# Two tiles of pair 0's exps turned by block transposes and transfers, a new search of the order, and 28 idle products in place of 16

## The chip, the cores and the metric

The kernel runs on one core of a Trainium2 chip. A time is the device time of one execution in microseconds; the value compared is the median of several runs. The engines are TensorE (PE), VectorE (DVE), ScalarE (ACT), GpSimd (POOL) and SyncE (SP), which issues most transfers.

## What is computed

Attention on 2 x 8 heads, then two expert layers, everything in 32-bit floats. Cut to what matters:

```python
def _attn_ref(q, k, v):                      # q, k, v: 2 x 8 x 1152 x 64
    q_pool = q.reshape(B, H, S // 2, 2, D).mean(axis=3)
    scores = scale * np.matmul(q_pool, k.transpose(0, 1, 3, 2))
    scores = scores - np.max(scores, axis=-1, keepdims=True)
    attn = np.exp(scores)
    attn = attn / (np.sum(attn, axis=-1, keepdims=True) + 1e-09)
    return np.matmul(attn, v)

def _moe_ref(x, w_in, w_out):                # 1152 x 512, 2048 wide
    h = x @ w_in
    return (np.maximum(h, 0.0) + np.log1p(np.exp(-np.abs(h)))) @ w_out

def _moe2_ref(x, w_gate, w_val, w_out, rms_g):   # 1536 wide
    xn = x / np.sqrt(np.mean(x * x, axis=-1, keepdims=True) + 1e-06) * rms_g
    g = xn @ w_gate
    return (g * (1.0 / (1.0 + np.exp(-g))) * (xn @ w_val)) @ w_out
```

## The kernel before

The sixteen heads are worked as eight pairs, 0 to 7, of heads A and B. After pooling a head has 576 queries: four tiles of 128 (x = 0 to 3) and half a tile; the half tiles of both heads make one mixed tile (x = 4, NF in the code). For each tile `qk` computes the scores against all 1152 keys (six matmuls of 384 columns, nine for the mixed tile), into one of two PSUM buffers, `sA` and `sB`: each head has one, so its next scores wait until the exps of the last are done. `softmax` takes the maximum of each row on VectorE (line 751) and the exps with their sum on ScalarE (line 753). A head's exps go into a ring of two buffers `p`.

The product with v (`av`, line 838) needs the exps with the keys on the partitions, so each tile is turned, in one of two ways. `flip` (line 773) transposes nine blocks of 128x128 for each head on TensorE, into the two-buffer ring `t` in PSUM, and ScalarE or VectorE copies them out (line 372 or 374). `stream` (line 810) does it for the tiles named in `STREAMS`: VectorE transposes each 128x1152 tile of exps in blocks of 32x32 into `turned`, and SyncE's queue then moves the blocks to their partitions in `moved`, in sixteen transfers (line 818) that are issued when the last of the pair's streamed tiles has been turned. The products of streamed tiles are put into the next pair (`before` in the main loop): tile 1 behind its tile 2, tile 3 behind its tile 3. Before the change pairs 1 to 5 stream tiles 1 and 3, pair 6 streams tile 1, pairs 0 and 7 none.

`heat` issues transposes of the identity that nobody reads: `WARM` of them at the start, `WAKE` behind the first scores (line 1286). `prep` loads, pools and splits a pair's q and k into high and low halves (`kk`, `kh`, `qh`, `ql`, `qm`), one pair ahead. The first weights of the expert layers are loaded and split during attention as well. `seven` and `expand` (line 953, 1019 to 1040) and `main_out` (line 1462) are the expert layers' matmuls.

Operations are recorded first (`plan.op`), each with the engines that may do it. The issue order and the engine of each stand in `ORDER`, a table that a search outside of the program wrote: `p46` is operation 46 on TensorE, `v3` operation 3 on VectorE, `a`, `g`, `s` stand for ScalarE, GpSimd and SyncE. `Plan.order` goes through this table and checks that each operation stands behind what it depends on. The durations beside the engines, as in

```python
def act(n, sbuf=True):
    return "ACT", n * 0.00096 + 0.15 if sbuf else n * 0.00085 + 0.155
```

served the search; the program itself uses only the engines' names.

Of the kernel before, what the change touches and what calls it, by code (L numbers as in the profile page):

```python
# [55 lines left out]
WAKE = 16  # L56
# [7 lines left out]
    a147 p152 a149 v79 v74 s214 p150 v75 p155 a151 s61 a156 p157 v83 v153 p159 a158 g221 p162 v160 p164 a154 g222 g223 v195 a161 s219 v239 v163 v235 s218 p186
    p188 v224 a165 a187 v225 p191 v240 v189 g237 p193 a192 p205 v226 a190 p209 v194 g231 v206 g230 p207 v210 g228 p212 a208 p246 a213 g232 a211 p249 v247 g236
    s332 s331 a241 v244 a248 s220 p251 v242 a233 g238 p254 v252 a250 p256 a255 g229 p259 a253 v257 g227 v260 a258 p265 v234 p261 v196 a171 p263 p288 a264 v266
    g338 s197 a262 g339 s217 p268 g337 v289 a269 s335 a243 p291 v245 a290 s330 s201 v270 s334 a267 p293 s198 v292 s199 p296 v294 a355 p298 s200 a297 p300 a299
    v271 a295 p303 v314 s278 v301 a168 p305 s279 p307 a306 s276 a304 v351 a302 p310 s282 p312 v308 g202 s286 g353 s277 a311 v313 s274 a309 p321 v315 p325 s275
    s280 v172 a322 p323 s281 v356 v326 g203 a324 p328 p362 s285 a329 g354 s283 p365 v363 a327 s273 g352 s287 s272 a364 v340 v341 s284 p367 g204 s316 g347 a342
    p372 v368 g346 a366 g344 p370 v373 p375 a371 g348 a376 p377 a369 v360 s320 s319 s317 v361 a374 p379 s479 p383 s478 v378 a380 s318 v416 p381 v343 p386 p406  # L70
    a387 v357 v384 g417 a382 p409 a359 v349 v407 g345 s477 v358 a408 v350 p411 v388 a410 p420 v485 a412 s333 a385 g484 s336 g415 g486 p423 v421 p425 g414 a424
    s481 a426 s482 p430 v389 p427 a422 v428 s396 a431 p452 s399 p454 a453 s390 v461 v169 a429 s400 p457 v455 p459 s405 a458 s392 v498 s398 p468 a460 a456 p470
    v502 s395 v413 p472 v469 g499 s397 a471 s391 p475 v473 p509 g501 a476 s402 s394 p512 g500 v510 a474 s393 s403 v462 a511 s404 p514 s401 v503 v489 s463 a418
    p517 v515 g492 a513 p519 a518 g490 p522 a516 v520 p524 v507 a523 s466 a487 v488 a521 p526 v494 p530 v525 g493 v508 a527 p528 p533 a529 p553 v531 g495 a534
    g491 a504 s601 a496 p556 v554 s467 a506 s602 s464 v505 a555 v170 s600 p558 v497 a557 v173 a532 v535 p563 s483 a180 s465 g608 p566 a559 v564 s480 p568 g607
    a567 p570 g609 a569 v536 s604 a565 p573 s605 v584 g174 s549 a625 v571 p575 a574 a178 s547 p577 g175 a576 s541 g562 v626 p580 a572 v578 g560 s539 p582 s550
    g561 s551 v581 a579 g176 p595 s542 v610 s543 p591 g179 v596 a182 p632 s548 a583 s544 v592 p593 g177 a597 s546 v633 p598 g181 s538 s540 a594 p637 v599 a621
    s537 g183 p635 s545 v638 s552 a634 v611 v617 p642 a636 v618 a639 v585 p640 p645 v643 g616 a641 p653 g624 s726 a646 s586 a184 p647 v630 a612 v419 a644 g185
    p649 v648 p651 v650 s588 a619 v654 p656 g614 s727 p676 a657 a652 s433 g623 s590 p679 a629 v677 s589 g615 s432 s587 v631 a678 p681 v613 a655 v620 v658 p688
# [1580 lines left out]
```

## Time and profile before

| | us |
|---|---|
| median of 3 runs | 650.23 (649.9 to 651.69) |
| the profiled execution | 647.97 |
| its span | 646.2 |
| TensorE busy | 628.1 (97%) |
| VectorE busy | 491.1 (76%) |
| ScalarE busy | 385.6 (60%) |
| GpSimd busy | 155.6 (24%) |

The span runs from the first to the last instruction in the profile; 1.8 us of the execution lie around it. The busy shares are means over stages of different kinds: attention until about 232 us, then the two expert layers, and 4 us of last copies and stores. "Idle before" in brackets behind a row is the time for which the engine waited, with what ended the wait as the profile infers it.

### The profile page before, as it was taken

How to read it: one execution, taken by the hardware profiler on the slowest of the kernel's cores; microseconds unless marked ns; L12 is line 12 of the kernel's file. 1: busy time of each engine (PE TensorE's matmuls, PEld its weight loads, DVE VectorE, ACT ScalarE, POOL GpSimd, SP SyncE). 2: the span in 40 equal slices, each digit the busy share in tenths (PEclk: the TensorE clock that was granted, in tenths of full speed). 3: DMA queues.
4: the chain of work that ended last, by engine and by line, in shares of the span. 5: the costliest groups of instructions: out<-in, count | busy, mean ns of one | idle time of the engine just before them, and what ended most of it. 6: DMA issues, size and time to landing. Idle time of an engine off the chain costs nothing.

```text
span 646.2 us, 10956 instructions
## 1 busy us (share of the span) xinstructions
PE 628.1 (97%) x4286; PEld 535.8 (83%) x4286; DVE 491.1 (76%) x695; ACT 385.6 (60%) x642; POOL 155.6 (24%) x160
## 2 busy tenths in 40 slices
PE   8998999899999999999999999999999999999997
PEld 7987888788888987888888888888888888888886
DVE  7799988989998788897886666878978877765111
ACT  6778777877877775675565554456365645533211
POOL 1442633643246241000001111301200101124201
PEclk9999999999999999999999999999999999999999
DMA  9246776968564214423141111111133133201004
GB/s 257 76 130 169 177 198 152 222 173 229 161 153 131 85 46 152 169 92 130 66 152 43 66 65 65 66 66 60 71 131 130 66 131 109 87 5 61 1 0 147
DMA packets 24850, 72.55 MB, mean 112 GB/s; under 512 B 5279, under 2 KB 6110, under 8 KB 24798
## 3 DMA queue, kind: packets, MB, share of 16 engines
q1 hardware_dynamic: 24222, 71.32, 36.9%
q8 instruction: 34, 0.56, 0.4%
q10 hardware_dynamic: 576, 0.53, 0.2%
q14 instruction: 18, 0.15, 0.1%
HBM read 56.46 MB, written 2.39 MB: 91 GB/s over the span
## 4 chain that ended last, share of the span: by engine, by line
PE 86%; DMA 4%; SPq 3%; ACT 3%; DVE 3%; issue 1%; ACTq 0%; DVEq 0%
PE s L953 24%; PE t L838 10%; PE s L1462 9%; PE s L737 9%; PE t L773 6%; PE t L953 5%; SPq L818 3%; PE s L1020 3%; PE s L1021 3%; PE s L1019 3%; PE t L1462 3%; PE s L1040 2%; PE t L1040 2%; PE t L1066 2%; ACT p L753 1%; PE s L1066 1%
## 5 line engine op out<-in xcount | busy, mean ns | idle before, releaser
L751 DVE TENSOR_REDUCE nm<-s 128x1 f32<-128x1152 f32 x72 | 96.7, 1349 | 17.7 <-PE s L737 14.7
L753 ACT ACTIVATE p<-s,nm 128x1152 f32<-128x1152 f32 x72 | 88.1, 1224 | 17.8 <-DVE nm L751 14.8
L372 ACT CAST areaLR<-areaKF 128x512 fp32r<-128x512 f32 (+2 forms) x55 | 44.4, 822 | 34.2 <-PE s L1462 12.0
L773 PE MATMUL t<-ident,p 128*128 128x128 f32 x378 | 55.7, 277 | 5.1 <-ACT p L753 4.0
L377 POOL TENSOR_TENSOR areaLR<-areaKF,areaLR 128x512 fp32r<-128x512 f32 (+1 forms) x9 | 13.1, 1455 | 173.3 <-ACT areaLR L372 150.4
L773 PEld LDWEIGHTS t<-ident,p 128*128 128x128 f32 x378 | 43.3, 140 | 13.2 <-ACT p L753 6.0
L442 ACT ACTIVATE areaKF<-areaKF 128x1024 f32<-128x1024 f32 (+1 forms) x37 | 39.8, 1079 | 20.6 <-DMA areaKF<-in_w2o_dram 5.1
L377 DVE TENSOR_TENSOR areaKF<-areaKF 128x256 f32<-128x256 f32 (+1 forms) x98 | 48.6, 513 | 2.2 <-ACT areaKF L1146 1.4
L372 ACT CAST areaMR<-areaKF 128x512 fp32r<-128x512 f32 (+1 forms) x37 | 26.6, 719 | 38.6 <-PE t L1462 17.1
L377 POOL TENSOR_TENSOR kk<-kr,kk 64x384 fp32r<-64x384 f32 x39 | 40.0, 1036 | 36.6 <-DVE kk L374 15.4
L453 DVE SCALAR_TENSOR_TENSOR areaKF<-areaKF 128x1024 int32<-128x1024 int32 (+1 forms) x37 | 41.8, 1133 | 3.7 <-ACT areaKF L442 3.3
L372 ACT COPY ptwhole<-t 128x512 f32<-128x512 f32 (+1 forms) x62 | 32.5, 546 | 14.1 <-PE t L773 13.6
L372 ACT CAST areaKR<-areaKF 128x1024 fp32r<-128x1024 f32 (+2 forms) x44 | 36.2, 840 | 6.0 <-DVE areaKF L453 4.7
L838 PE MATMUL t<-areaKF,v 128*64 128x128 f32 x576 | 34.7, 274 | 4.5 <-ACT ptwhole L372 2.0
L953 PE MATMUL s<-areaKR,areaLR 128*128 128x512 f32 x132 | 38.2, 395 | 0.0
L953 PE MATMUL s<-areaKR 128*128 128x512 f32 x130 | 37.9, 397 | 0.0
L838 PEld LDWEIGHTS t<-areaKF,v 128*64 128x64 f32 x576 | 31.5, 137 | 7.0 <-ACT ptwhole L372 2.4
L953 PE MATMUL s<-areaMR,areaKR 128*128 128x512 f32 x134 | 36.9, 393 | 0.0
L377 DVE TENSOR_TENSOR areaLR<-areaKF,areaLR 128x1024 fp32r<-128x1024 f32 (+2 forms) x29 | 29.5, 1028 | 8.3 <-ACT areaLR L372 8.1
L838 PE MATMUL t<-ptwhole,v 128*64 128x128 f32 x576 | 35.0, 275 | 0.0
L838 PEld LDWEIGHTS t<-ptwhole,v 128*64 128x64 f32 x576 | 31.1, 137 | 3.5 <-issue 2.5
L377 DVE TENSOR_TENSOR areaLR<-areaKF,areaMR 128x512 fp32r<-128x512 f32 (+1 forms) x21 | 17.5, 837 | 19.9 <-ACT areaMR L372 19.9
(286 smaller groups left out, 1590.7 us busy)
## 6 DMA issues: line engine op xcount, KB each, us to landing
areaKF<-areaKF SPq DMA_DIRECT2D x80, 144.0 KB, 3.0
areaKF<-in_w_dram SPq DMA_DIRECT2D x16, 512.0 KB, 5.4
areaKF<-in_w1o_dram SPq DMA_DIRECT2D x16, 512.0 KB, 4.6
qr<-in_qT_dram SPq DMA_DIRECT2D x28, 288.0 KB, 4.7
areaKF<-in_wv_dram SPq DMA_DIRECT2D x12, 512.0 KB, 4.1
areaKF<-in_wg_dram SPq DMA_DIRECT2D x12, 512.0 KB, 3.8
areaKF<-in_w2o_dram SPq DMA_DIRECT2D x12, 512.0 KB, 4.2
v<-in_v_dram SPq DMA_DIRECT2D x16, 288.0 KB, 5.2
```

The costliest lines, as they stand in the source:

```text
L372: nc.scalar.copy(out, in_)
L377: engines[e].tensor_tensor(out=out, in0=in0, in1=in1, op=o)
L442: o = op([act(n)], lambda e, x0=x0, x1=x1: nc.scalar.activation(out=word(1, x0, x1).bitcast(F32), in_=word(1, x0, x1).bitcast(F32), scale= ...
L453: op([dve(n)], lambda e, x0=x0, x1=x1: nc.vector.scalar_tensor_tensor(out=word(1, x0, x1), in0=word(1, x0, x1), scalar=3, in1=word(0, x0, ...
L737: nc.tensor.matmul(sc()[:, c, :N], lhsT=q()[:, cut], rhs=k()[:, c * N:(c + 1) * N], start=(i == 0), stop=(i == len(todo) - 1))
L751: u["mx"] = op([dve(S, psum=True)], lambda e: nc.vector.tensor_reduce(out=nm(), in_=sc()[:, :, :N], axis=AX.XY, op=ALU.max, negate=True), ...
L753: o = op([("ACT", 1.42)], lambda e: nc.scalar.activation(out=pr(), in_=sc()[:, :, :N], func=AF.Exp, bias=nm(), accum_out=s["den"]()[:, col ...
L773: nc.tensor.transpose(t()[:, i * P:(i + 1) * P], pr[:, c * P:(c + 1) * P], ident)
L838: nc.tensor.matmul(t()[h * D:h * D + D, :n], lhsT=s["v"][h]()[:, c, :], rhs=rhs, start=(c == 0), stop=(c == CK - 1))
L953: nc.tensor.matmul(bank(), lhsT=a(k), rhs=b(k), start=start and k + i == 0, stop=stop and k + i == 3, skip_group_check=seeded)
L1040: nc.tensor.matmul(out, lhsT=x()[:, cut], rhs=w[:, k], start=k + i == 0, stop=k + i == KC + 1)
L1462: nc.tensor.matmul(out[m](), lhsT=w, rhs=g(), start=j + i == 0, stop=last and j == js[-1] and i == 2)
```

## The change

Pair 0 now streams its tiles 1 and 3 as pairs 1 to 5 do. 36 transposes on TensorE (378 to 342 at line 773) and ten evictions go; four block transposes on VectorE (22 to 26 at line 810) and sixteen transfers of 144 KB (80 to 96 at line 818) come; the products of these two tiles move into pair 1. `WAKE` goes from 16 to 28. The durations for ScalarE and GpSimd are written anew, the third entry of two VectorE durations goes, and `ORDER` is another table throughout: GpSimd has 23 operations more (165 to 188 instructions), of which eight are in the attention stage. The `(3,)` in `STREAMS` and `old[0]` in place of 1 have no effect on the program, since pair 0 is in `DOUBLE` and the one pair with a single streamed tile has tile 1.

```diff
-DOUBLE = (1, 2, 3, 4, 5)
-STREAMS = {pb: (1, 3) if pb in DOUBLE else (1,) if pb else () for pb in range(NP)} | {NP - 1: ()}
+DOUBLE = (0, 1, 2, 3, 4, 5)
+STREAMS = {pb: (1, 3) if pb in DOUBLE else (1,) if pb else (3,) for pb in range(NP)} | {NP - 1: ()}
...
-WAKE = 16
+WAKE = 28
...
-    p46 v3 s10 q11 v8 v4 s12 v7 q13 a45 v9 v5 s14 s15 s16 v20 v21 s17 v2 a22 v6 s18 a28 v23 s19 v29 p48 a24 a44 v25 p47 v26 v27 p49 a32 v34 a30 p54 v50 a35 s57
...
 def act(n, sbuf=True):
-    return "ACT", n * 0.00096 + 0.15 if sbuf else n * 0.00085 + 0.155
+    return "ACT", n * 0.00083 + 0.2 if sbuf else n * 0.00085 + 0.155
...
 def pool(n):
-    return "POOL", 0.05 + n * 0.00275
+    return "POOL", 0.18 + n * 0.0022
...
-            op([("DVE", 1.37, 1)], lambda e, h=h, pr=pr: nc.vector.transpose(
+            op([("DVE", 1.37)], lambda e, h=h, pr=pr: nc.vector.transpose(
...
-        op([("DVE", 0.93, 1)], lambda e: nc.vector.reciprocal(sums(), sums()), w=[(sums, None)])
+        op([("DVE", 0.93)], lambda e: nc.vector.reciprocal(sums(), sums()), w=[(sums, None)])
...
-            before = [(pb - 1, t) for t in when.get(x, ())] if len(old) == 2 else [(pb - 1, 1)] if old and x == 1 else []
+            before = [(pb - 1, t) for t in when.get(x, ())] if len(old) == 2 else [(pb - 1, old[0])] if old and x == 1 else []
```

**TensorE, the first tiles of pair 0**, behind the first scores. Before, p_206 and p_213 are the exps of tile 0 (heads A and B), p_257 those of tile 1 of head A; kk_148 and kk_153 are the keys of heads A and B:

```order
L1286 MATMUL t<-ident 128x128 x16
L773 MATMUL t<-ident,p_206 128x128 x4
L737 MATMUL s<-kk_148,qhA_146 128x384 x3
L737 MATMUL s<-kk_148,qlA_211 128x384 x3
L773 MATMUL t<-ident,p_206 128x128 x4
L773 MATMUL t<-ident,p_213 128x128 x8
L773 MATMUL t<-ident,p_206 128x128
L773 MATMUL t<-ident,p_213 128x128
L737 MATMUL s<-kk_153,qhB_128 128x384 x3
L737 MATMUL s<-kk_153,qlB_255 128x384 x3
L773 MATMUL t<-ident,p_257 128x128 x8
L737 MATMUL s<-kk_148,qhA_146 128x384 x3
```

After the change the same place reads (tile 0 is p_215 and p_238, the keys are kk_144 and kk_148):

```order
L1286 MATMUL t<-ident 128x128 x28
L773 MATMUL t<-ident,p_215 128x128 x4
L737 MATMUL s<-kk_144,qhA_125 128x384 x3
L737 MATMUL s<-kk_144,qlA_213 128x384 x3
L773 MATMUL t<-ident,p_215 128x128 x4
L773 MATMUL t<-ident,p_238 128x128 x4
L737 MATMUL s<-kk_148,qhB_127 128x384 x3
L737 MATMUL s<-kk_148,qlB_241 128x384 x3
L773 MATMUL t<-ident,p_238 128x128 x4
L773 MATMUL t<-ident,p_215 128x128
L773 MATMUL t<-ident,p_238 128x128
L737 MATMUL s<-kk_144,qhA_125 128x384 x3
```

The eight transposes of tile 1 are gone; the scores of tile 2 of head A follow directly on tile 0's transposes, and the idle products are twelve more.

**VectorE, the middle of pair 0**, from the reduction of tile 2 of head B on. Before, nm_351 is that reduction, nm_376 and nm_433 are those of tile 3 (A and B), nm_463 that of the mixed tile:

```order
L751 TENSOR_REDUCE nm_351<-s 128x1
L751 TENSOR_REDUCE nm_376<-s 128x1
L374 COPY O<-t 128x128
L699 TENSOR_SCALAR qhA_150<-qs 128x512
L633 SCALAR_TENSOR_TENSOR qlA_419<-qs,qhA_150 128x512
L656 SCALAR_TENSOR_TENSOR qm_131<-qs,qhA_150 64x64
L751 TENSOR_REDUCE nm_433<-s 128x1
L751 TENSOR_REDUCE nm_463<-s 128x1
```

After, the same four reductions are nm_338, nm_365, nm_409 and nm_436; p_266 and p_290 are the exps of tile 1, p_384 those of tile 3 of head A:

```order
L751 TENSOR_REDUCE nm_338<-s 128x1
L810 STREAM_TRANSPOSE areaKF<-p_266 128x9x4x32
L751 TENSOR_REDUCE nm_365<-s 128x1
L810 STREAM_TRANSPOSE areaKF<-p_290 128x9x4x32
L633 SCALAR_TENSOR_TENSOR qlA_394<-qs,qhA_131 128x512
L656 SCALAR_TENSOR_TENSOR qm_133<-qs,qhA_131 64x64
L751 TENSOR_REDUCE nm_409<-s 128x1
L751 TENSOR_REDUCE nm_436<-s 128x1
L810 STREAM_TRANSPOSE areaKF<-p_384 128x9x4x32
```

Block transposes stand in front of both reductions of tile 3; a copy and the rounding of q have moved to other places or engines.

**VectorE, from pair 2 to pair 3.** Before, nm_1147 is the reduction of pair 2's mixed tile, nm_1201 and nm_1228 are pair 3's first two, p_1189 are the exps of pair 2's tile 3 of head B, the last of its streamed tiles:

```order
L751 TENSOR_REDUCE nm_1147<-s 128x1
L656 SCALAR_TENSOR_TENSOR qm_131<-qs,qhB_126 64x64
L633 SCALAR_TENSOR_TENSOR qlB_522<-qs,qhB_126 128x512
L810 STREAM_TRANSPOSE areaKF<-p_1078 128x9x4x32
L377 TENSOR_TENSOR qs<-qr 128x224
L751 TENSOR_REDUCE nm_1201<-s 128x1
L810 STREAM_TRANSPOSE areaKF<-p_1189 128x9x4x32
L751 TENSOR_REDUCE nm_1228<-s 128x1
```

After (nm_1123 is the mixed tile, nm_1183 and nm_1202 are pair 3's first two, p_1125 are the exps of tile 3 of head B):

```order
L751 TENSOR_REDUCE nm_1123<-s 128x1
L374 CAST kh<-kr 128x1152
L633 SCALAR_TENSOR_TENSOR qlB_461<-qs,qhB_457 128x512
L810 STREAM_TRANSPOSE areaKF<-p_1125 128x9x4x32
L810 STREAM_TRANSPOSE areaKF<-p_1067 128x9x4x32
L751 TENSOR_REDUCE nm_1183<-s 128x1
L751 TENSOR_REDUCE nm_1202<-s 128x1
```

Both block transposes now stand ahead of pair 3's first reduction. It is so from pair 2 to 3, 3 to 4, 4 to 5 and 5 to 6; from pair 1 to 2 the first reduction still stands between the last two.

## Rows read from the trace of the kernel before

**Rows 1.** Busy by stretch: start:end, length, busy (instructions) by engine, granted clock, DMA

```profile
7.30:10.56 3.26, 2.01 (x19) 1.73 (x17) 3.26 (x4) 2.11 (x6) 2.20 (x2) 1.00 1.07 262
10.56:29.46 18.90, 18.66 (x172) 17.24 (x173) 15.57 (x23) 13.91 (x27) 4.94 (x7) 1.00 0.53 155
...
10.56:232.48 221.92, 210.31 (x2258) 191.35 (x2259) 194.97 (x241) 171.00 (x311) 92.59 (x108) 1.00 0.60 157
232.48:642.55 410.07, 409.80 (x1983) 337.94 (x1981) 288.00 (x433) 207.42 (x320) 60.12 (x44) 1.00 0.24 85
```

**Rows 2.** Chain of waits, 46 to 64 us (pair 1): start, length, what

```profile
46.27 2.12 PE t L838 x36
48.38 1.28 PE s L737 x6
...
49.69 1.37 DVE nm L751
...
51.08 1.32 ACT p L753 x2
...
53.79 0.87 PE t L773 x8
54.66 1.59 PE s L737 x9
...
58.59 0.71 issue
```

**Rows 3.** Groups of instructions by shape, 0 to 245 us: busy, mean ns, idle before

```profile
L810 DVE STREAM_TRANSPOSE areaKF<-p 128x1152 f32<-128x1152 f32 x22 | 29.8, 1367 | 0.8 <-issue 0.6
...
L374 DVE COPY ptwhole<-t 128x512 f32<-128x512 f32 x14 | 9.6, 684 | 1.5 <-PE t L773 1.5
...
L372 ACT COPY areaKF<-t 128x512 f32<-128x512 f32 x15 | 8.4, 590 | 3.9 <-PE t L773 3.9
```

**Rows 4.** Timeline of TensorE around the idle products: start, length, what, idle before

```profile
7.34 1.97 PE L1286 MATMUL t<-ident 128*128 128x128 f32 x16
10.56 0.66 PE L773 MATMUL t<-ident,p 128*128 128x128 f32 x4 [1.25 <-ACT p L753]
```

**Rows 5.** Timeline of TensorE: two waits for exps, pairs 1 and 4

```profile
52.45 0.81 PE L737 MATMUL s<-kk,qhB 128*128 128x384 f32 x3 [0.86 <-ACT p L753]
...
118.15 0.66 PE L773 MATMUL t<-ident,p 128*128 128x128 f32 x4 [0.71 <-ACT p L753]
```

**Rows 6.** Timelines: one issue of sixteen transfers, the first products that read such transfers

```profile
63.30 10.58 SPq L818 DMA_DIRECT2D areaKF<-areaKF  x16
...
76.48 2.19 PE L838 MATMUL t<-areaKF,v 128*64 128x128 f32 x36 [0.88 <-ACT ptwhole L372]
...
103.89 2.19 PE L838 MATMUL t<-areaKF,v 128*64 128x128 f32 x36 [1.19 <-DMA row<-sums]
...
133.13 2.19 PE L838 MATMUL t<-areaKF,v 128*64 128x128 f32 x36 [0.40 <-ACT areaKR L372]
...
187.62 2.19 PE L838 MATMUL t<-areaKF,v 128*64 128x128 f32 x36 [1.12 <-ACT ptwhole L372]
```

**Rows 7.** Timeline of VectorE: first reductions of pairs 3, 4 and 6

```profile
87.89 1.36 DVE L751 TENSOR_REDUCE nm<-s 128x1 f32<-128x1152 f32 x1 [1.04 <-PE s L737]
...
115.33 1.36 DVE L751 TENSOR_REDUCE nm<-s 128x1 f32<-128x1152 f32 x1 [0.52 <-PE s L737]
...
171.68 1.36 DVE L751 TENSOR_REDUCE nm<-s 128x1 f32<-128x1152 f32 x1 [0.30 <-PE s L737]
```

**Rows 8.** Timelines of VectorE and GpSimd: a slow tensor_scalar, its neighbour, an ordinary one

```profile
82.46 0.41 DVE L699 TENSOR_SCALAR qhB<-qs 128x512 fp32r<-128x512 f32 x1
...
121.75 1.31 POOL L377 TENSOR_TENSOR areaKR<-areaKF,areaKR 128x512 fp32r<-128x512 f32 x1
...
121.77 1.58 DVE L699 TENSOR_SCALAR qhA<-qs 128x512 fp32r<-128x512 f32 x1
```

More of the change, by code (lines that the diff above doesn't have):

```diff
@@ L64 @@
[L64 to L79, printed above, removed]
@@ new lines @@
+    p145 v81 a121 v123 g71 a76 g72 p148 g73 v146 a124 g79 s209 s208 v127 g77 a147 v78 a149 p150 v74 a84 v75 p153 v151 s207 p155 a154 p157 a156 v128 a152 p160
+    v191 s144 v161 a164 p182 v158 s136 p187 a183 p184 s131 a188 v82 s141 v168 a159 p189 s139 v83 v185 g215 s132 g214 p198 a190 s134 p202 a186 v199 s143 v219
+    s129 p200 p205 s137 v203 p239 g221 a206 s140 a201 g216 s135 p242 v240 a204 s130 s138 v166 a241 s133 v192 p244 s142 a228 s211 v243 p247 v8 v245 s193 p249
+    a248 g231 s212 a232 p252 a246 v233 p254 v250 g220 a253 g229 v237 s194 a217 g222 s196 a174 p256 p260 s195 v255 a251 v257 s197 p258 v218 p263 p283 v224 a264
@@ new lines @@
+    v261 g223 a259 g225 p286 g230 s331 a236 v284 s332 g175 a226 s330 v238 a285 p288 v227 a262 v234 v265 p293 s210 a287 s213 a289 p296 v294 p298 a297 p300 a299
+    v266 a295 p303 v301 s274 a304 p305 s278 p307 a306 s276 v314 a302 v342 p310 s271 p312 v235 s270 v308 g338 a311 s268 g290 p321 s273 v313 a309 p325 g339 v322
+    s275 g337 s269 p323 v291 a355 p328 s280 v326 g292 a324 p362 g343 s277 a329 p365 s272 v363 a327 s279 s282 v356 a364 v315 s281 p367 s267 v351 a167 s335 p370
+    v366 g353 a340 s316 v368 p372 a371 g352 s334 p375 v373 a369 p377 g354 v360 a376 g344 s319 s318 p379 v341 a378 p383 a374 s320 v380 g346 s317 g347 v361 p381
@@ new lines @@
+    g445 v878 a448 g443 v907 a858 p913 g863 a912 a446 p915 v914 p917 g449 a916 v879 a450 p920 p922 g447 a908 v833 s895 s885 g451 v918 a921 a869 s834 p924 p926
+    s977 v859 a925 s976 v940 a923 a919 v874 s888 v871 p929 s889 p931 v927 g864 g872 s835 a930 s836 a928 v865 s837 g861 p956 s880 v932 p958 a957 v866 s884 p962
+    v959 a867 s883 v868 s894 p960 p965 a961 s851 v870 p967 a966 v963 s891 p969 a968 s838 a875 p972 s854 a964 v970 p974 s890 s886 v997 a973 s892 a971 s893 p988
+    v975 p990 s887 v989 g933 a938 s882 v979 p993 s881 p995 v991 g934 a994 g941 a877 p1004 v996 p1006 v1005 a992 g939 p1008 v1007 p1011 v998 g935 p1013 a1012
@@ L141 @@
+    a2220 p2217 v2221 p2213 p2222 a2226 p2223 g2227 p2248 p2229 p2251 p2218 p2224 p2228 p2230 a2232 v2234 p2219 s2233 v2236 p2225 s2235 p2231 p2254 v2238 s2239
+    p2257 s2237 a2258 v2260 q2259 s2261
 """
```

131 lines of the change are left out of this document (67 added, 64 removed).

## The prediction

> **What bounds the kernel now.** I read the busy times by stretch first. From 232.48 to 642.55 us (the two expert layers) TensorE is busy for 409.80 of 410.07 us [rows 1]: there is nothing to win, and a lead that the attention stage hands over arrives at the end undiminished. From 10.56 to 232.48 us (attention) TensorE is busy for 210.31 of 221.92 us, idle for 11.6, with VectorE at 194.97 close behind [rows 1]. So attention is TensorE's work plus 11.6 us in which it waits, and the change is worth what it takes from either. The granted clock is 1.00, the upper level of 2.4 GHz, in all these stretches [rows 1].
>
> Then the chain of waits in pair 1, for what TensorE waits for. A head has one score buffer, so its next scores wait for a round: scores 1.28, reduction 1.37, exps 1.32, 4.0 us in all with the steps between [rows 2]. TensorE fills that round with the other head's scores, with transposes (0.87 for eight) and with the products with v (2.12 for one tile) [rows 2]. Where too little of that stands between two scores of a head, it idles.
>
> **Transposes leave TensorE.** Tiles 1 and 3 of pair 0 have nine blocks for each of two heads, 36 transposes. At 0.87 for eight [rows 2] that is 36 x 0.109 = 3.9 us, and since TensorE has hardly an idle moment around it (0.24 us between 10.56 and 29.46 [rows 1]), the whole is on the path: -3.9.
>
> With them go ten evictions (eight of 512 columns, two of 256). In come four block transposes, 1.37 us each on VectorE, against 0.59 for such an eviction on ScalarE and 0.68 on VectorE [rows 3]. VectorE gains about 5.5 us and loses about half the evictions, some 2.5; it stood at 15.57 of 18.90 us there [rows 1], so it just fits if the order is kind. That is costed below, as idle time of TensorE.
>
> The Trainium skill speaks against this trade: the page "VectorE: DVE Perf Modes", under "Rules for kernel authors", gives a 128x128 transpose to TensorE where PSUM will do as its target, and its table in "The three transpose paths" has 390 ns for it. By that figure 36 would be worth an estimated 14.0 us and the time 636; the row has 0.109 us for one, so the sum doesn't use it.
>
> **Twelve more idle products.** The sixteen of before start at 7.34 and end at 9.31; TensorE then idles for 1.25 us until the first exps come [rows 4]. At 1.97/16 each, twelve more last 1.5 us, at the transposes' 0.109 they last 1.3. They hide behind those exps, and what sticks out is 0 to 0.25; I take 0.1, nearer to the back-to-back rows. Below nothing it can't go: the clock that they could raise is already 1.00 there [rows 1]. If the first exps came earlier, they would stand in the way in full, 1.3.
>
> **Pair 0 as a ramp.** This is the term against the change. Pairs 1 to 5 fill the gaps of their streamed tiles with the previous pair's streamed products; pair 0 has no previous pair. From the first transposes to the mixed scores TensorE now has six scores (1.06 each: nine take 1.59), 36 transposes (3.9), one product (2.1) and the nine mixed matmuls (1.6): 14.0 us. The round gives three times 4.0 plus the mixed scores, 13.6 [rows 2]. The two are equal, so anything late shows. In the new VectorE order the block transposes of tile 1 stand ahead of the two reductions of tile 3, and those of tile 3 ahead of pair 1's first ones. Following the new orders instruction by instruction with the durations of rows 2 and 3, I find TensorE idle for 1.0 us before the transposes of tile 2 of head B, 0.65 before the mixed scores, 1.0 before pair 1's first scores and 0.8 before its first transposes: 3.45. The sixteen transfers of pair 0 can add 0 to 1.2 (next part); I take 0.6.
>
> Against it: the product of tile 1 now stands in pair 1 where TensorE waited 0.86 us for exps [rows 5], that of tile 3 where it waited 0.71 with no releaser shown [rows 2], and the 0.24 of pair 0 are counted already: 1.8 goes. Net 3.45 + 0.6 - 1.8 = +2.2. The bounds: 0 to +1 if the round is filled as well as it is in pair 1 (0.24 idle before); +5.5 if all four block transposes (4 x 1.37) fall on the path.
>
> **Late transfers.** The last block transpose of a pair releases sixteen transfers; SyncE's queue issues them in 10.58 us and the product that reads them can start 13.2 us after the first (63.30 to 76.48) [rows 6]. It is late in four of five pairs: TensorE waited 0.88, 1.19, 0.40 and 1.12 us there [rows 6], 3.6 together (the releasers named had mostly ended long before). The new order puts the last block transpose ahead of the next pair's first reduction in pairs 2 to 5, so the transfers start 1.3 us earlier or more; pair 1's stands as before. That takes 1.19 + 0.40 + 1.12 = 2.7. The price: that reduction comes later, by up to 1.37, less VectorE's idle time just before it, 1.04, 0.52 and 0.30 in three of the four [rows 7]: 4 x 1.37 - 1.86 = 3.6 at most. TensorE has little to spare there: it already waits up to 0.71 us for these exps [rows 5]. So between -2.7 and +0.9; I take -1.0, just below the middle, because VectorE's idle time before the reduction is seen in three of four places.
>
> **Everything else.** The whole order was searched anew, and some 23 small operations go from VectorE and ScalarE to GpSimd. In the expert layers 0.27 us of idle time [rows 1] is all there is to win, so it is 0 or a loss; I take 0, and +1.5 as the bound.
>
> **The sum** on the profiled execution: span 646.2 - 3.9 + 0.1 + 2.2 - 1.0 = 643.6, with the 1.8 us around the span 645.4 in place of 647.97. That execution is 2.3 us below the median of the runs, 650.23; taken from the median, -2.6 gives 647.6.
>
> **The rivals.**
> 1. *The ramp is filled and the waits go.* If pair 0 idles no more than pair 1 did (net 0) and 3.6 us of transfer waits end at no price: -7.5, 642.7. For it: VectorE has idle time in pair 0. Against it: the round and TensorE's work are equal there, with no slack.
> 2. *The ramp eats the gain.* With five and a half us in pair 0 less the 1.8, and nothing won at the boundaries: -3.9 + 3.7 + 0.1 = -0.1, 650.1. For it: TensorE's 0.24 us of idle time in pair 0 come from work that is now taken out. A stall in the expert layers would do the same to a smaller gain.
> 3. *GpSimd holds VectorE.* A VectorE tensor_scalar of 128x512 took 1.58 us where its like takes 0.41, while GpSimd ran a tensor_tensor from 121.75 to 123.06 [rows 8]: 1.17 us lost. Eight of the operations that move to GpSimd lie in the attention stage. If four of them meet such an instruction with VectorE on the path, +4.7 less the 2.6: 652.3; with two, 649.9. The Trainium skill's page "SBUF — State Buffer", under "Who interferes with whom", gives a reason: the two engines share one pair of ports, and whichever starts first holds it for its whole instruction; the row agrees. Against it: they also take work off VectorE.
> 4. *Reductions queue behind block transposes* (slower). Each of pair 0's four block transposes stands ahead of a reduction, 5.5 us, and the four boundaries cost 3.6. With all of it on TensorE's path: -3.9 - 2.7 + 5.5 + 3.6 + 0.1 = +2.6, 652.8. It decides once more than seven tenths of those 9.1 us reach TensorE. For it: five of TensorE's longer waits are for exps, and two of them stand in the rows [rows 5]. Against it: VectorE's idle time in front of the reductions [rows 7].
>
> **How the numbers follow.** Forecast 0.50 (its own range 646 to 648.8), rival 1 0.13, rival 2 0.17, rival 3 0.07, rival 4 0.13. About 0.3% (2 us) is what a measurement of this kernel can tell from no change. The forecast is faster by more with 0.43 of its 0.50, rival 1 with all: 0.56. Within 0.3%: 0.07 of the forecast, rival 2, and 0.05 of rival 3: 0.29. Slower: rival 4 and the rest of rival 3, 0.15. The range, 643.5 to 652.0, takes in rivals 2 and 3 mostly, and half of rival 1 and a third of rival 4.
>
> **What would show it.** In the changed profile: 342 transposes at line 773; TensorE idle for 3 to 5 us between 10.5 and some 40 us, waiting for exps; the product with tile 1 of pair 0 starting 13 us after its first transfer, with at most 1.2 us of waiting; the waits of 1.19, 0.40 and 1.12 gone in pairs 2, 3 and 5, those for the next pair's first exps longer by up to a microsecond; the expert layers at 410 us. I am wrong on the ramp if that idle time is under 2 or over 6 us, on the boundaries if both waits shrink or both grow, and on the cover of the whole if the expert layers take more than 411 us.

## The result and the profile after

The changed kernel takes 644.29 us (642.49 to 646.54, 4 runs) against 650.19 us: ratio 0.9913 [0.9888, 0.9939], 0.9% or some 5.7 us faster. A second series (below) gives 0.9919 [0.9896, 0.9941]. The forecast was 647.6, faster by 2.6; the range 643.5 to 652.0 holds the result, but the gain is about twice the forecast's.

The profiled executions tell less than the runs: 647.97 before, 644.73 after, so 3.2 us, and spans of 646.2 and 642.9. I take the spans apart first and come back to the rest.

Busy time by stretch. The cuts are the first transposes of pair 0, the mixed scores of pair 2, those of pair 6, the first expert product, and the end; columns as in [rows 1]. Before:

```profile
10.56:81.84 71.28, 67.85 (x680) 61.94 (x681) 63.25 (x81) 55.09 (x100) 30.00 (x37) 1.00 0.58 153
81.84:195.70 113.86, 106.55 (x1173) 96.50 (x1173) 102.11 (x120) 88.69 (x163) 46.36 (x56) 1.00 0.72 182
195.70:232.48 36.78, 35.91 (x407) 32.91 (x407) 29.61 (x41) 27.21 (x50) 16.23 (x16) 1.00 0.30 89
232.48:646.20 413.72, 409.80 (x1983) 337.94 (x1981) 288.43 (x434) 207.79 (x321) 60.12 (x44) 1.00 0.24 85
```

After:

```profile
10.98:80.44 69.46, 63.87 (x644) 58.23 (x645) 63.89 (x82) 55.26 (x99) 29.17 (x37) 1.00 0.70 182
80.44:193.90 113.46, 105.31 (x1173) 96.70 (x1173) 99.17 (x118) 86.74 (x155) 58.16 (x71) 1.00 0.75 187
193.90:229.13 35.23, 35.20 (x403) 32.52 (x403) 28.54 (x42) 27.56 (x49) 10.52 (x11) 1.00 0.33 94
229.13:642.90 413.77, 409.97 (x1987) 338.31 (x1985) 288.65 (x417) 206.24 (x322) 83.14 (x59) 1.00 0.24 85
```

| part of the span | before | after | difference | forecast |
|---|---|---|---|---|
| up to the first transposes | 10.56 | 10.98 | +0.42 | +0.1 |
| pairs 0 and 1, to pair 2's mixed scores | 71.28 | 69.46 | -1.82 | -1.7 (-3.9 + 2.2) |
| pairs 2 to 6 | 113.86 | 113.46 | -0.40 | -1.0 |
| the last pair, to the first expert product | 36.78 | 35.23 | -1.55 | 0 |
| expert layers and end | 413.72 | 413.77 | +0.05 | 0 |

Pair 0 came out as forecast: TensorE's busy time fell by 3.98 us and its idle time grew by 2.16 (71.28 - 67.85 before, 69.46 - 63.87 after), where -3.9 and +2.2 were said. Pairs 2 to 6 won a little less than the forecast, and not by its mechanism: TensorE's idle time grew there, from 7.31 to 8.15, and what was won is busy time, 1.24 us less for the same 1173 instructions in another order. The last pair, to which the prediction gave nothing, won half of it all. The expert layers took nothing, with fifteen GpSimd operations more in them (44 to 59, busy 60.12 to 83.14).

TensorE around the ramp (start, length, what, idle before), the answer to [rows 2, 4]:

```profile
7.26 3.28 PE L1286 MATMUL t<-ident 128*128 128x128 f32 x28
10.98 0.66 PE L773 MATMUL t<-ident,p 128*128 128x128 f32 x4 [0.44 <-ACT p L753]
...
23.09 0.66 PE L773 MATMUL t<-ident,p 128*128 128x128 f32 x4 [0.96 <-ACT p L753]
...
25.80 0.79 PE L737 MATMUL s<-kk,qhA 128*128 128x384 f32 x3 [0.32 <-ACT p L753]
...
30.55 0.77 PE L737 MATMUL s<-kk,qhA 128*128 128x384 f32 x3 [0.77 <-ACT p L753]
...
34.84 1.09 PE L773 MATMUL t<-ident,p 128*128 128x128 f32 x8 [0.83 <-ACT p L753]
...
47.66 2.19 PE L838 MATMUL t<-areaKF,v 128*64 128x128 f32 x36 [0.79 <-DMA areaKF<-areaKF]
```

Four waits for exps, 2.9 us, at the four places that the prediction named (1.0, 0.65, 1.0, 0.8); it had said 3 to 5 us until some 40 us. The product with tile 1 starts 13 us after pair 0's first transfer (34.70) and waits 0.79, where 0 to 1.2 was allowed.

The boundaries, pairs 2 to 5, with the issues of three pairs' transfers, those of pairs 1, 2 and 5 (the answer to [rows 5, 6]):

```profile
101.96 2.19 PE L838 MATMUL t<-areaKF,v 128*64 128x128 f32 x36 [0.62 <-DMA areaKF<-areaKF]
...
116.21 0.66 PE L773 MATMUL t<-ident,p 128*128 128x128 f32 x4 [0.71 <-ACT p L753]
...
129.47 2.19 PE L838 MATMUL t<-areaKF,v 128*64 128x128 f32 x36 [1.27 <-DMA areaKF<-areaKF]
...
178.50 2.18 PE L838 MATMUL t<-ptwhole,v 128*64 128x128 f32 x34 [1.32 <-DMA v<-in_v_dram]
...
185.84 2.19 PE L838 MATMUL t<-areaKF,v 128*64 128x128 f32 x36 [1.98 <-ACT qhA L697]
```

```profile
61.77 10.80 SPq L818 DMA_DIRECT2D areaKF<-areaKF  x16
...
85.24 0.81 SPq L383 DMA_DIRECT2D v<-in_v_dram  x2
86.38 12.92 SPq L818 DMA_DIRECT2D areaKF<-areaKF  x16
...
166.81 1.18 SPq L818 DMA_DIRECT2D areaKF<-areaKF  x2
168.10 0.52 SPq L383 DMA_DIRECT2D kr<-in_kT_dram  x1
168.67 0.69 SPq L818 DMA_DIRECT2D areaKF<-areaKF  x1
169.40 0.58 SPq L383 DMA_DIRECT2D v<-in_v_dram  x1
170.03 13.13 SPq L818 DMA_DIRECT2D areaKF<-areaKF  x13
```

Pair 2's transfers in the kernel before, for comparison:

```profile
87.64 1.12 SPq L383 DMA_DIRECT2D qr<-in_qT_dram  x2
90.57 10.80 SPq L818 DMA_DIRECT2D areaKF<-areaKF  x16
```

The waits for streamed tiles did not go: 0.62, 1.27, 0 and 1.98 in pairs 2 to 5 against 1.19, 0.40, 0 and 1.12 before. The transfers of these four pairs do start earlier, 4.8 to 5.9 us after the pair's mixed scores where it was 8.7. But from the first transfer to the product that reads them it is 15.6, 16.4, 16.2 and 19.0 us, where it was 13.3, 15.1, 12.9 and 13.3. In the kernel before, the last load ahead of them had been issued 1.8 us or more before the first transfer; now loads are issued within the last microsecond ahead of it or among the sixteen. Pair 5's sixteen transfers, with two loads among them, are issued in 16.3 us, where pair 1's take 10.8. A wait of 1.32 us for a load of v, at 178.50, is new and stands in no forecast; after_again (below) does not have it. The waits for the next pair's first exps are 0.70 to 0.71 in all four, where three of them were 0.24 or 0.25.

### The profile page after: what moved, and what is told of

Same layout as the page of the kernel before. It is cut to its first block, busy times and chain, and to the rows that moved or that the text cites. A ratio compares the mean times of both kernels' runs of the same rounds, so it can differ in the third digit from the quotient of the medians.

```text
span 642.9 us, 10926 instructions
## 1 busy us (share of the span) xinstructions
PE 623.5 (97%) x4262; PEld 533.5 (83%) x4262; DVE 487.8 (76%) x674; ACT 383.0 (60%) x634; POOL 182.7 (28%) x183
## 4 chain that ended last, share of the span: by engine, by line
PE 82%; DMA 7%; DVE 4%; SPq 4%; ACT 2%; issue 1%; ACTq 0%; DVEq 0%
PE s L953 25%; PE s L1462 10%; PE t L838 9%; PE s L737 7%; PE t L953 5%; PE t L773 4%; SPq L818 3%; PE s L1019 3%; PE s L1021 3%; PE s L1020 3%; DMA v<-in_v_dram 3%; PE t L1462 3%; PE t L1040 2%; PE s L1040 2%; PE t L1066 2%; DVE nm L751 2%
## 5 line engine op out<-in xcount | busy, mean ns | idle before, releaser
L751 DVE TENSOR_REDUCE nm<-s 128x1 f32<-128x1152 f32 x72 | 96.8, 1348 | 11.0 <-PE s L737 9.6
L372 ACT CAST areaLR<-areaKF 128x512 fp32r<-128x512 f32 (+2 forms) x57 | 45.9, 818 | 30.8 <-DVE areaKF L453 10.1
L377 DVE TENSOR_TENSOR areaKF<-areaKF 128x256 f32<-128x256 f32 (+1 forms) x99 | 54.8, 578 | 3.3 <-ACT areaKF L1146 1.5
L773 PE MATMUL t<-ident,p 128*128 128x128 f32 x342 | 50.0, 277 | 5.8 <-ACT p L753 5.8
L377 POOL TENSOR_TENSOR kk<-kr,kk 64x384 fp32r<-64x384 f32 x40 | 40.1, 1010 | 36.5 <-issue 12.4
L773 PEld LDWEIGHTS t<-ident,p 128*128 128x128 f32 x342 | 39.2, 140 | 12.5 <-ACT p L753 8.1
L377 POOL TENSOR_TENSOR areaLR<-areaKF,areaMR 128x512 fp32r<-128x512 f32 x14 | 20.6, 1470 | 97.4 <-ACT areaMR L372 42.2
L453 DVE SCALAR_TENSOR_TENSOR areaKF<-areaKF 128x1024 int32<-128x1024 int32 (+1 forms) x37 | 44.3, 1203 | 5.0 <-ACT areaKF L442 4.4
L372 ACT CAST areaKR<-areaKF 128x1024 fp32r<-128x1024 f32 (+2 forms) x45 | 37.0, 826 | 13.2 <-DVE areaKF L453 6.8
L377 POOL TENSOR_TENSOR qs<-qr 128x224 f32<-128x224 f32 (+1 forms) x38 | 23.0, 627 | 59.7 <-DVE qm L656 22.5
L372 ACT COPY ptwhole<-t 128x512 f32<-128x512 f32 (+1 forms) x60 | 30.8, 538 | 13.0 <-PE t L773 12.4
L377 POOL TENSOR_TENSOR areaLR<-areaKF,areaLR 128x512 fp32r<-128x512 f32 x10 | 14.5, 1446 | 81.2 <-ACT areaLR L372 63.9
L377 DVE TENSOR_TENSOR areaLR<-areaKF,areaLR 128x1024 fp32r<-128x1024 f32 (+3 forms) x28 | 30.0, 1075 | 7.7 <-ACT areaLR L372 7.2
```

The lines of the kernel that those rows point to most:

```text
L372: nc.scalar.copy(out, in_)
L377: engines[e].tensor_tensor(out=out, in0=in0, in1=in1, op=o)
L453: op([dve(n)], lambda e, x0=x0, x1=x1: nc.vector.scalar_tensor_tensor(out=word(1, x0, x1), in0=word(1, x0, x1), scalar=3, in1=word(0, x0, ...
L751: u["mx"] = op([dve(S, psum=True)], lambda e: nc.vector.tensor_reduce(out=nm(), in_=sc()[:, :, :N], axis=AX.XY, op=ALU.max, negate=True), ...
L773: nc.tensor.transpose(t()[:, i * P:(i + 1) * P], pr[:, c * P:(c + 1) * P], ident)
```

## Where the last pair won: VectorE behind GpSimd

VectorE and GpSimd (start, length) of the kernel before in pair 7, then the product that waits on TensorE:

```profile
200.06 1.45 DVE L699 TENSOR_SCALAR qhB<-qs 128x512 fp32r<-128x512 f32 x1
201.54 1.22 DVE L633 SCALAR_TENSOR_TENSOR qlB<-qs,qhB 128x512 fp32r<-128x512 f32 x1
202.69 1.34 DVE L751 TENSOR_REDUCE nm<-s 128x1 f32<-128x1152 f32 x1
203.96 0.67 DVE L374 COPY ptmixed<-t 128x512 f32<-128x512 f32 x1
```

```profile
199.91 1.31 POOL L377 TENSOR_TENSOR areaKR<-areaKF,areaKR 128x512 fp32r<-128x512 f32 x1 [1.37 <-ACT areaKR L372]
201.18 1.04 POOL L377 TENSOR_TENSOR areaKF<-areaKF 128x256 f32<-128x256 f32 x1
```

```profile
204.68 2.19 PE L838 MATMUL t<-areaKF,v 128*64 128x128 f32 x36 [0.85 <-DVE ptmixed L374]
```

The scaling takes 1.45 in place of 0.41 [rows 8], the next operation 1.22 in place of 0.69, both while GpSimd is at work; 1.6 us late, VectorE frees the PSUM bank that TensorE's product needs. After, the scaling and the copy are ScalarE's and GpSimd is idle until 200.61; TensorE goes through without a wait:

```profile
198.25 0.64 ACT L697 ACTIVATE qhB<-qs 128x512 fp32r<-128x512 f32 x1
199.94 1.27 ACT L372 COPY ptmixed<-t 128x512 f32<-128x512 f32 x2
```

```profile
201.79 2.19 PE L838 MATMUL t<-areaKF,v 128*64 128x128 f32 x36
```

That is 0.85 of the 1.55. Another 0.4 is four transposes that stood ahead of the first expert product and now stand behind it, where the expert layers took no longer (413.77). The remaining 0.3 was not traced.

## Experiments

Most of these are hybrids. An operation has a number in each kernel, so one kernel's operations can be put in the other's order from some place on. "Changed" is the changed kernel.

**The changed kernel once more**, to see whether the medians or the profiles mislead.

> The changed kernel once more, since its medians say -5.9 us and its profiled execution only -3.3 us against the profiled execution of before. Theory A (the profile is right; the three runs of before happened to lie high): the ratio moves to about 0.995 (-3.3 us) and runs of before come down to 648. Theory B (the runs are right: executions of before differ in how late the transfers of the streamed tiles land, and the profiled one was a lucky one): the ratio stays near 0.991 (-5.9 us), before stays at 650.

644.49 us, ratio 0.9919; its profile repeats the stretches above (69.40, 112.99, 35.24, 413.78). The 23 runs of before beside it have their median at 649.13 and go from 647.56 to 651.94; over all series it is 649.6 in 89 runs. So the profiled 647.97 was a quick execution, four of the 89 lie below it: theory B in its size, though runs of before do come down to 648. Against 649.6, ten runs of the changed kernel (median 644.5) are 5.1 us faster.

**Pair 0 alone, the later order alone.**

```diff
 # pair0_alone: changed kernel, ORDER from pair 2's first scores (p293) on as in the kernel before
-    p293 s210 a287 s213 a289 p296 v294 p298 a297 p300 a299 v266
+    p293 v287 p296 v294 a355 p298 a297 p300 a299 v266
 # order_alone: the kernel before, ORDER from the same place on as in the changed kernel
-    p293 s198 v292 s199 p296 v294 a355 p298 s200 a297
+    p293 a292 p296 v294 p298 a297 p300 a299 v271 a295
```

> The changed kernel with pair 0's two tiles through block transposes and transfers and with the new order up to pair 2's first scores; everything from there stands in the order of before. In the profile of after TensorE is 1.5 us ahead at that place and 3.35 us ahead at the first expert product. Theory 1 (parts add up, pair 0 is worth what the ramp leaves): -1.5 us against before, ratio 0.998. Theory 2 (pair 0 carries it all, the later order is worth nothing): -3.3 to -5.9 us, ratio 0.995 to 0.991. Theory 3 (the ramp eats it; all is won later): 0, ratio 1.000.

> The kernel before, pair 0 with its transposes and in its old order up to pair 2's first scores; everything from there stands in the new order (block transposes ahead of reductions at the pair boundaries, GpSimd's additional operations, the new expert layers). Theory 1 (parts add up): -1.9 us by the profile, up to -4.4 us if the runs are right, ratio 0.997 to 0.993. Theory 2 (the later order is worth nothing): ratio 1.000. Theory 3: all of the gain, 0.995 to 0.991.

Pair 0 alone: 0.9997 [0.9979, 1.0014]. Order alone: 0.9973 [0.9954, 0.9993], 1.8 us faster. Together 2.0 of 5.1 us: they do not add up, and the profiles show why. Where the two orders meet there is a seam. TensorE in pair0_alone, then in order_alone:

```profile
62.98 0.66 PE L773 MATMUL t<-ident,p 128*128 128x128 f32 x4 [1.26 <-ACT p L753]
...
77.37 2.19 PE L838 MATMUL t<-areaKF,v 128*64 128x128 f32 x36 [2.42 <-ACT p L753]
```

```profile
63.42 0.66 PE L1248 MATMUL t<-ident,p 128*128 128x128 f32 x4 [1.58 <-ACT O L372]
```

From pair 1's mixed scores to pair 2's, pair0_alone takes 29.3 us (changed: 27.4), order_alone 27.1 (before: 26.3). With these seams of 1.9 and 0.9 taken out, an estimate, the parts are -2.1 and -2.7, 4.8 together: theory 1 fits, but the seam correction is read, not run.

**The idle products**, in both directions.

```diff
 # after_16_idle: changed kernel          # before_28_idle: kernel before
-WAKE = 28                                -WAKE = 16
+WAKE = 16                                +WAKE = 28
```

> The changed kernel with 16 idle products behind the first scores in place of 28, nothing else. Theory 1 (they hide behind the first exps): within 0.2 us of the changed kernel, the first transposes again at 10.98 us. Rival (they stand in the way of the first transposes, which are 0.42 us later than before): 0.4 us faster than the changed kernel. Rival (they raise something later): slower by a microsecond or more.

> The kernel before with 28 idle products in place of 16, nothing else; its profile is also a second look at the order of before. Theory 1 (they hide behind the first exps): 0 us, ratio 1.000, first transposes between 10.4 and 11.1 us as in all profiles so far. Rival (they are worth something by themselves): over 1 us faster. Its waits for streamed products tell how far before's profile, 1.2 us under the median of 26 runs, was a lucky one: if so they add up to more than the 4.4 us of the first profile (0.88, 1.19, 0.40, 1.12, 0.85).

0.9922 [0.9897, 0.9948] and 1.0015 [0.9997, 1.0033]: nothing either way. With sixteen, the changed kernel's first transposes start at 11.53, no earlier than with 28 (10.98 and 11.09), so the idle products are not what delays them. before_28_idle is a second look at before's order: 71.82, 114.84 and 36.76 us in the stretches, and its waits of that list come to 7.1 us (0.86 in pair 7 again) where the first look had 4.4. Its 648.79 lies nearer to the median of 649.6: in these waits the first look was a lucky one.

**The last pair alone, and all but the last pair.**

```diff
 # tail_alone: kernel before, from pair 6's mixed scores (p926) on as in the changed kernel
-    p926 s885 a923 v863 a925 s887 g442 a938
+    p926 s977 a925 s976 v940 a923 s888 p929
 # no_tail: changed kernel, from there on as in the kernel before
-    p926 s977 v859 a925 s976 v940 a923 a919
+    p926 a923 a925 s887 a938 s894 p929 v927
```

> The kernel before up to the mixed scores of pair 6 (195.7 us), from there everything in the new order (pair 7, expert layers). In all three profiles of the changed order the stretch from there to the first expert product takes 35.2 us, in before 36.8. Theory (the new order of the last pair is worth this by itself): -1.5 us, ratio 0.9977. Rival (it needs the lead of the earlier pairs): 0, ratio 1.000.

> The changed kernel up to the mixed scores of pair 6, from there everything in the order of before. If the last stretch is worth 1.55 us and the parts add up: 1.55 us slower than the changed kernel, ratio to before 0.9943. Rival (a seam, or no effect of its own): 0.9919 like the changed kernel, or over 3 us slower.

no_tail: 0.9943 [0.9924, 0.9962], the number forecast for parts that add up, 1.4 us of the gain gone. Its profile does not bear that reading out: the last stretch takes 35.78, only 0.55 more than in the changed kernel, and pairs 2 to 6 take 114.92 there, with a wait of 2.95. The interval reaches that of the changed kernel, so the number may be chance. tail_alone: 0.9989 [0.9971, 1.0007], less than the 1.5; its last stretch takes 36.03, 0.75 less than before, and a wait of 0.50 at the seam takes a part. no_tail's profile also tells the cause. Its 35.78 are one microsecond less than the same order took before (36.78 and 36.76), and GpSimd runs at other times there: it is idle from 200.22 to 205.70. VectorE, the same two operations:

```profile
200.88 0.43 DVE L699 TENSOR_SCALAR qhB<-qs 128x512 fp32r<-128x512 f32 x1
201.34 0.69 DVE L633 SCALAR_TENSOR_TENSOR qlB<-qs,qhB 128x512 fp32r<-128x512 f32 x1
```

0.43 and 0.69 in place of 1.45 and 1.22, and the product behind them starts without a wait (204.14). Of the 1.55 us, about one is thus the collision with GpSimd.

**The pulled block transposes put back.**

```diff
 # blocks_behind: last block transpose behind the next pair's first reduction (pair 3; pairs 2, 4, 5 alike)
-    a555 v536 a506 p563 s483 v497 s480 a559 p566 v564 a180 s552
+    a555 a506 p563 s483 v497 s480 a559 p566 v564 v536 a180 s552
```

> The changed kernel with one edit undone: the last block transpose of pairs 2 to 5 stands behind the next pair's first reduction on VectorE again, with the transfers that it releases. The prediction's theory (an earlier start of the transfers is worth 1.0 us net): 1.0 us slower than the changed kernel; the waits for the next pair's first exps go from 0.70 to 0.24 in up to four places (-1.8), the streamed products wait 1.4 us longer in up to four (+5.5 at most). Rival (the transfers are paced by what else the DMA engines carry and land no earlier): the streamed products wait no longer, and the kernel is 0 to 1.8 us faster.

658.2 us, 1.0132 [1.0105, 1.0158]: 13.7 us slower than the changed kernel, outside of both expectations. VectorE and the transfers at pair 3's end:

```profile
114.54 1.36 DVE L751 TENSOR_REDUCE nm<-s 128x1 f32<-128x1152 f32 x1 [1.26 <-PE s L737]
115.81 1.37 DVE L810 STREAM_TRANSPOSE areaKF<-p 128x1152 f32<-128x1152 f32 x1
117.11 0.65 DVE L374 COPY ptmixed<-t 128x512 f32<-128x512 f32 x1
```

```profile
117.21 3.08 SPq L818 DMA_DIRECT2D areaKF<-areaKF  x5
```

The reduction waits for scores of its own, and the block transpose with it. Counted from the pair's mixed scores the transfers start 8.7 us later, as before the change; in the changed kernel it is 5.7. So pulling ahead is worth 3.0 us of lead here (2.8 to 3.9 in the four pairs) and not the 1.3 of a reduction. Pair 2 shows that a later start need not cost that much: with the loads of v four microseconds ahead, its product starts 13.3 us after the first transfer (89.78 to 103.09), 15.6 in the changed kernel. The copy of the mixed tile now waits too: TensorE's first transposes of the next pair wait 1.26 to 1.66, not the expected 0.24. And the longest waits cost twice. TensorE at pair 5's product, and the stretch in which it runs (the third number from the end is the granted clock):

```profile
198.66 3.85 PE L838 MATMUL t<-areaKF,v 128*64 128x128 f32 x36 [4.30 <-DMA qr<-in_qT_dram]
```

```profile
198.60:202.60 4.00, 3.94 (x37) 3.81 (x38) 1.21 (x1) 0.06 (x1) 0.83 (x1) 0.57 0.01 5
```

After 4.30 us without work the product takes 3.85 in place of 2.19, at a granted clock of 0.57 of 2.4 GHz in the mean, so mostly at the lower of the two levels, 1.2 GHz. The changed order depends on that place; how much the old order would win by it was not run.

**One more pulled, one load moved.** Pair 1's last block transpose was not pulled ahead by the change, and pair 5's transfers have a load of 576 KB (k) and one of 288 KB (v) among them.

```diff
 # pull_pair1
-    p296 v294 p298 a297 p300 a299 v266
+    p296 v266 v294 p298 a297 p300 a299
 # kr_behind: order on SyncE's queue; s848 loads pair 7's k, s731 the second half of pair 6's v
-    s728 s799 s796 s848 s797 s731 s789 ... s795
+    s728 s731 s799 s796 s797 s789 ... s795 s848
 # and VectorE's cast of it: v860 behind s848; pull_and_kr_later: behind the next block transpose, v878, and reduction, v907
```

> The changed kernel with one more block transpose pulled ahead: the last of pair 1 stands in front of pair 2's first reduction on VectorE, as in pairs 2 to 5. The product with pair 1's streamed tiles waits 0.8 to 1.1 us in every profile of the changed order. Theory (earlier transfers are what the boundaries win): that wait goes, at up to 0.5 us for the later reduction: 0.5 to 1.0 us faster than the changed kernel, ratio to before 0.991 to 0.990. Rival (the reduction is late and TensorE's wait of 0.7 us for these exps grows by the 1.37 us of the transpose): 0.5 us slower.

> The changed kernel with the load of pair 7's k (576 KB) behind the sixteen transfers of pair 5 instead of among them, its cast on VectorE and one subtraction on GpSimd moved back accordingly, and the second load of pair 6's v two transfers earlier. In four profiles the product with pair 5's tiles waits 2.0 to 2.3 us, and the transfers take 17 us there where they take 10.7 elsewhere. Theory (the transfers go at the rate at which the DMA engines carry everything in the queue, 2.3 MB in 10.6 us, so 576 KB ahead of them cost 2.7 us): that wait goes, 2 us faster than the changed kernel, ratio to before 0.989. Rival (they wait for something else): 0. Rival (pair 7's k comes late): slower by over a microsecond, waits before pair 7's first scores at 198 us.

> Both edits on the changed kernel: the last block transpose of pair 1 pulled ahead, and pair 7's k loaded behind the transfers of pair 5. If both theories hold and add up: 2.5 to 3 us faster than the changed kernel, ratio to before 0.987 to 0.988. If neither does: 0.992.

> As the run with both edits, but the cast of pair 7's k on VectorE stands three reductions later, behind the first block transpose of pair 6's tile and the reduction after it, where VectorE has 1.8 us to spare: in the run before, the cast waited 6.8 us for the load with two reductions queued behind it. The sixteen transfers took 10.2 us there without the 576 KB among them, against 17 us. Theory (the transfers are paced by what the DMA engines carry ahead of them): TensorE's wait of 2.0 to 2.3 us for pair 5's product goes and none takes its place, 2 us faster than with the pulled transpose alone, ratio to before 0.987. Rival (the load lands too late for the cast even there, or the product waits as before): 0.990 to 0.994.

pull_pair1: 644.15 us, 0.9903 [0.9882, 0.9923]. Pair 1's product no longer waits, the transposes before it wait 1.13 in place of 0.72, and the span is 641.5. From pair 1's mixed scores to pair 2's the profile has 26.6 us, where two profiles of the changed kernel have 27.4 and 27.2. The runs do not show this step: the medians differ by 0.1 to 0.3 us and the intervals overlap.

kr_behind and pull_and_kr: 1.0008 and 0.9980, a loss of 4 to 6 us, by my placing of the cast: VectorE waits for the load with two reductions queued behind it (6.82 us in kr_behind). With the cast later, pull_and_kr_later: 643.42 us, 0.9907 [0.9889, 0.9925], no better than pull_pair1. SyncE's queue in kr_behind, VectorE's wait, and the queue in pull_and_kr_later:

```profile
169.73 10.21 SPq L818 DMA_DIRECT2D areaKF<-areaKF  x16
```

```profile
187.57 0.75 DVE L374 CAST kk<-kr 64x1152 fp32r<-64x1152 f32 x1 [6.82 <-DMA kr<-in_kT_dram]
```

```profile
167.40 10.28 SPq L818 DMA_DIRECT2D areaKF<-areaKF  x16
```

Without the load of k among them, and with the loads of v ahead of them, the sixteen transfers go out in 10.2 and 10.3 us. With the loads among them it was 16.3 and 16.4 us in two profiles but 12.0 and 12.4 in two others, and the wait was 2.0 to 2.3 us in all four, so the time of issue alone does not set the wait. The time from the first transfer to the product says more: 16.1 us in pull_and_kr_later, 17.5 to 19.0 in those four. Pair 5's product waits 1.12 us. The gain is lost a little later, in the same way as in the kernel before. VectorE and GpSimd in pull_and_kr_later:

```profile
191.43 1.32 DVE L656 SCALAR_TENSOR_TENSOR qm<-qs,qhA 64x64 fp32r<-64x64 f32 x1
192.78 1.57 DVE L377 TENSOR_TENSOR kk<-kr,kk 64x384 fp32r<-64x384 f32 x1
```

```profile
188.93 5.00 POOL L377 TENSOR_TENSOR areaKR<-areaKF,areaKR 128x512 fp32r<-128x512 f32 x3
```

Two operations that take 0.21 and 0.55 elsewhere take 1.32 and 1.57 beside GpSimd's, the reduction behind them is 2.1 us late, TensorE waits 0.89 us at 196.29, and the last pair's stretch takes 36.7 in place of 35.2. In the changed kernel GpSimd's work at this place ends 1.9 us before the first of the two operations (191.68 and 193.58). So no version found here is clearly better than the changed kernel.

## Why the prediction was right, and where it fell short

**Right: TensorE bounds it, the lead arrives whole.** The expert layers took 413.7 us in both; what attention won, 3.35 us of lead at the first expert product, is the 3.3 of the spans.

**Right: pair 0.** 342 transposes at line 773, as forecast. Idle time at the four forecast places (2.9 us for 3.45), the transfers 0.79 late (forecast 0.6), the two older waits gone: -1.82 for -1.7. Both of its terms held, -3.98 of busy time for -3.9 and +2.16 of idle time for +2.2. Rival 1 (a filled ramp) and rival 2 (a ramp that eats the gain) both fall. Hybrid runs alone do not show it: pair0_alone is no faster than before. Its profile is 2.1 us ahead of before's at pair 1's mixed scores (53.45 and 55.57), and with the estimated seam taken out its runs agree with about 2 us.

**The idle products: right in size, wrong in the place.** Bounds 0 to 0.25, and the runs show nothing. The start is 0.42 later for another reason: VectorE comes to its first reduction at 8.23 and not at 7.81, behind a fourth subtraction in place of a shorter cast, and a wait for the load of q that is 0.1 longer. The prediction had read the start of the new order on TensorE alone.

**The boundaries: the sign held by luck, the terms did not.** The prediction said it would be wrong if both kinds of wait grew, and in the profile both did: the first exps by 0.46 in three places (the forecast price, up to 1 us), the streamed products from 2.7 to 3.9 us in pairs 2 to 5. The earlier start, 1.3 us in the prediction, was 2.8 to 3.9. What failed is the step from there to the wait: it took the 13.2 us from the first transfer to the product as fixed, and they became 15.6 to 19.0 when the transfers started just behind loads, or with loads among them. That the loads are the cause is seen in pair 2 (13.3 in blocks_behind, where the transfers start later) and in part in pair 5 (16.1 in pull_and_kr_later); pairs 3 and 4 were not run. In pair 3 the product was moved forward as well, ahead of the scores of head B (1.3 us) behind which it stood before; in the other three pairs it keeps its place. That the stretch is shorter all the same comes from a term that the prediction did not have: TensorE's busy time for the same products is 104.79 to 105.31 us in four profiles of the changed order (a fifth, after_16_idle, has a fall of the clock in it) and 106.45 to 106.59 in four of before's. Which changes of order do that was not run. In five profiles of the changed order this stretch took 111.49 to 114.92 us (113.4 in the mean), in four of before's 113.48 to 114.84 (114.1). The -1.0 lies within that spread and is not settled better than to a microsecond.

**Wrong: "0 or a loss" for everything else.** This is the step that failed. It was argued for the expert layers alone, where it held, and then used for the rest of the search as well, which it did not cover. The evidence was there: the trace of before has a wait of 0.85 us at 204.68, which the prediction's list of late products left out, with a VectorE operation of 1.45 us ahead of it. I had put the same collision into [rows 8] and into rival 3, but only as something that the change might add. A price that lies in the trace of before can be taken away by a new order as well as added. Last pair: -1.55 for 0.

**Rival 3 and rival 4.** Rival 3 is refuted as a whole: with more work on GpSimd VectorE lost less time to it. Its `qhA` scalings took 415 ns in the mean (three) where they took 695 (five); and of all its instructions in the attention stage 8 and 6 took over 0.15 us longer than the shortest of their shape in the two profiles of the changed kernel, 15 and 15 in the two of before's order. Its mechanism is real, though, as before (1.45), no_tail (0.43) and pull_and_kr_later (1.57 for 0.55) show. The Trainium skill's page "SBUF — State Buffer" adds, under "Who interferes with whom", that a VectorE operation with two inputs in SBUF is held up by GpSimd's reads and a reduction never is; the rows agree, since the subtraction went from 0.55 to 1.57 and the 72 reductions of the attention stage keep a mean of 1348 ns (1349 before). Rival 4 is refuted: the reductions came later, but TensorE's waits for the first exps grew by 0.46 each, nowhere near the 9.1 us in all.

**Why 5.1 us in the runs and 3.2 in the profiles.** The forecast worked its 2.6 out on an execution that was itself 1.6 below the median of 89 runs, and then took them from a median. Part of the remainder is thus chance in one profile. What differs between executions of before could be seen in a long one, tail_alone's profile (649.9 us span), which follows before's order up to pair 6. TensorE, and the stretch:

```profile
11.65 0.75 PE L773 MATMUL t<-ident,p 128*128 128x128 f32 x4 [1.98 <-ACT p L753]
12.06 1.30 PE L737 MATMUL s<-kk,qhA 128*128 128x384 f32 x3
```

```profile
11.65:32.03 20.38, 20.36 (x172) 18.83 (x173) 15.63 (x23) 13.94 (x27) 5.21 (x7) 0.92 0.53 137
```

The first exps came a microsecond later, TensorE stood idle for 1.98 us, and its next scores took 1.30 in place of 0.77, at the lower clock: pair 0 took 20.38 us in place of 18.9. In kr_behind, with 28 idle products, the exps came as late (11.87) and pair 0 took its usual 15.9. That would be a use of the twelve products, but the runs with 16 and 28 do not bear it out, so it stays open, as does whether before's executions lose more to late loads than the changed kernel's.

## What to carry to other kernels

Price a collision or a wait that the trace of before already contains as something a new order can remove, not only as a risk that it may add: go through all waits of the bounding engine, and ask of each whether the changed order still has it. Of a transfer that is started earlier, ask what else the queue carries in that time and whether its reader has been moved forward too; the wait shown is then no measure of the gain. Compare busy time and idle time of the bounding engine apart: a stretch can get shorter while its waits grow. And know where in the spread of the runs the one profiled execution lies before a forecast is taken from its rows.

## What was not expected of the hardware

- The clock after a wait. In all profiles here, waits of TensorE up to 2.4 us in mid-attention were followed by a product of the usual 2.19 us; after one of 2.95 it also took 2.19, after 2.82, 2.97, 3.36 and 4.30 it took 3.54, 3.66, 3.85 and 3.85, for the most part at the lower level. At the start of pair 0, 1.98 us were followed by the lower level too (tail_alone). So a late transfer can cost some 1.5 us beyond its wait. The Trainium skill's page "TensorE: Matmul & The Clock Gate" ("What's actually happening") has the clock fall after idleness and return with activity; these rows agree, and in blocks_behind the granted clock is 1.00 again from 202.60 to 204.00 us.
- Sixteen transfers of 144 KB between partitions were issued in 10.6 to 11.0 us in the kernel before, where no load was issued in the last microsecond ahead of them or among them (some 220 GB/s, an estimate from their bytes and this time). With such loads it was 10.2 to 16.4 us over all profiles. The time until they can be read is another matter: with the loads just ahead and an issue of 10.3 us, the product of pair 5 started 16.1 us after the first transfer and had waited 1.12 us (pull_and_kr_later); in before it was 13.3.
- How long a VectorE instruction takes depends on the microsecond: the same two operations in the same order took 1.45 and 1.22 us, or 0.43 and 0.69, by what GpSimd did at that moment.
